# Gate and value products of a gated layer's second token half by Strassen's seven products, with their combinations on GpSimd

## Chip, cores and metric

The kernel runs on one core of a Trainium2 chip. The metric is the device time of one launch in microseconds (us); the kernel before takes 1157.8 us (median of three runs, 1156.64 to 1159.02). Engines go by the profile's names: PE (TensorE matmuls), PEld (its weight loads), DVE (VectorE), ACT (ScalarE), POOL (GpSimd) and SP (SyncE, which here only issues DMAs).

## What is computed

Attention over 4 x 12 heads of 448 x 64, then a layer of eight experts with a sorted routing, then a gated layer. The change is in the last one; its input x has 1792 tokens of 768.

```python
def _moe2_ref(x, w_gate, w_val, w_out) -> np.ndarray:
    gate = 1.0 / (1.0 + np.exp(-(x @ w_gate)))
    val = x @ w_val
    return (gate * val @ w_out).astype(np.float32)
```

The gate and value matrices are 768 x 1536, the output matrix is 1536 x 768.

## The kernel before, in words

**Precision.** A float32 operand is split in a high and a low part of a format that PE reads fast. `prods` takes a list of pairs of such operands and issues three matmuls for each (high x high, high x low, low x high), all into one PSUM bank. The operand ahead in a pair is stationary (128 x 128), the other streams (448 tokens, or 384 output columns).

**Gated layer.** `moe2(hf)` runs twice, for a half of 896 tokens each, that is two blocks of 448. For each of `NF` = 12 weight blocks `f` (128 columns of gate and of value) and each token block it makes the gate by 18 matmuls (6 depth tiles x 3) into a bank `pg`, ACT's sigmoid `gv`, the value by 18 matmuls into `pv`, DVE's product (L875), and the high and low part of that product `h` in `hx` (ACT L877, DVE L878). After every second `f` comes the output stage: for 7 token tiles and two column halves each 6 matmuls of 384 columns (3 for each of the two `f`), and DVE adds the bank to `acc` (L899; for the first pair ACT copies it). At the last pair GpSimd scatters the rows to the output.

**Weights.** `load_chunk` brings the weights in the order of the list `chunks`: gate and value of one `f` are one chunk ("gv"), the output weights of two `f` another ("wo"). A chunk's high and low part lie in `wh` and `wl`, four buffers each. In the first half the inputs are 64-bit numbers: `conv_half` loads half a chunk (`cs`, two buffers), ACT and DVE turn it into float32 (`ca`, two buffers, DVE L87 to L92) and split it (ACT L93, DVE L94), and SP stores both parts in a DRAM scratch `wsc` (L711, L712). In the second half SP only reads them back (L708, L709).

**Second half's tokens.** They come out of the experts as float32 (`X2F`), and `split2` splits them (ACT L914, DVE L915) at the end of the first half.

**Order.** PE's order is that of the code. The order on the other engines is made at build time by a scheduler; each engine executes its own list strictly in that order, and SP's DMAs are issued in SP's. PSUM has seven banks `g` for this part. Buffers rotate, and a writer waits until the last reader of the buffer's earlier content has ended.

```python
            for bb in range(2):
                x2h, x2l = X2[2 * hf + bb]
                xx = [(x2h[:, d, :], x2l[:, d, :]) for d in range(KD)]
                pg = ps.tile([128, 512], F32, name="g", bufs=7)
                prods(pg[:, :448], list(zip(wv[:KD], xx)))
```

Of the kernel before, what the change touches and what calls it, by code (L numbers as in the profile page):

```python
# [7 lines left out]
F32 = mybir.dt.float32  # L8
# [14 lines left out]
KD = 6  # L23
# [7 lines left out]
def body(ctx: ExitStack, tc: tile.TileContext, q, k, v, moe_w_gate, moe_w1, moe_w2,  # L31
# [12 lines left out]
    x_d = dram.tile([N, DM], F32, name="x_d")  # L44
    idx_d = dram.tile([N, 1], I32, name="idx_d")
# [19 lines left out]
    def conv_half(kind, f, n, hn, ln):  # L65
        cs = cv.tile([128, HC, 2], U32, name="cs", bufs=2)
        with tc.issue_after(xst[-1]):
            conv_load(kind, f, n, cs)
        conv_split(cs, hn, ln)
# [8 lines left out]
    def conv_split(cs, hn, ln):  # L78
# [15 lines left out]
        nc.vector.tensor_tensor(ln, w_, hn.bitcast(F32), op=OP.subtract)  # L94

# [573 lines left out]
    WB = 4  # L669

    def load_chunk():
# [3 lines left out]
        if kind in ("w1", "w2") and a in SPLIT:  # L675
            wh_, wl_ = (mp.tile([128, CH], F32R, name=n, bufs=WB) for n in ("wh", "wl"))
# [9 lines left out]
        if kind in ("w1", "w2"):  # L686
            full = mp.tile([128, CH], F32, name=("wh", "wl")[stream["next"] % 2], bufs=WB)
# [11 lines left out]
        hi = mp.tile([128, CH], F32R, name="wh", bufs=WB)  # L699
        lo = mp.tile([128, CH], F32R, name="wl", bufs=WB)  # L700
        o_ = wsc[wsc_n[kind, c]]
        for n in range(2):
            cc = slice(n * HC, (n + 1) * HC)
            if a == 0:
                with tc.issue_after(marks[E - 2].ins):
                    conv_half(kind, c, n, hi[:, cc], lo[:, cc])
# [3 lines left out]
        if a == 0:  # L710
# [3 lines left out]
        stream["next"] += 1  # L714

# [71 lines left out]
    def moe(ph, nxt):  # L787
# [35 lines left out]
        if half == 0:  # L823
            if blk < 2:
                X2[blk] = [mp.tile([128, KD, 448], F32R, name=n, bufs=2) for n in ("x2h", "x2l")]
            else:
                X2F[blk] = mp.tile([128, KD, 448], F32, name="x2f", bufs=2)
        xo = slice(half * CAP, (half + 1) * CAP)
        ws = [use(("w2", ph, c)) for c in range(2)]
        for dp in range(0, KD, 2):  # L830
# [25 lines left out]
    def moe2(hf):  # L856
        NT = 7
# [3 lines left out]
        for f in range(NF):  # L861
            wh, wl = use(("gv", hf, f))
# [3 lines left out]
            for bb in range(2):  # L866
                x2h, x2l = X2[2 * hf + bb]
                xx = [(x2h[:, d, :], x2l[:, d, :]) for d in range(KD)]
# [7 lines left out]
                gv = pv[:, :448]  # L876
                nc.scalar.activation(hx[:, 0, bb], gv, AF.Copy)  # L877
                nc.vector.tensor_tensor(hx[:, 1, bb], gv, hx[:, 0, bb].bitcast(F32), op=OP.subtract)  # L878
            gs.append(hx)
            if f % 2 == 1:  # L880
                oh, ol = use(("wo", hf, f - 1))
                if f == NF - 1:
                    nc.gpsimd.dma_start(idxf, idx_d[hf * 896:(hf + 1) * 896].rearrange("(t p) o -> p (t o)", p=128))
                    if hf == 0:
                        split2()
                for tt in range(NT):
                    for dh in range(2):
                        po = ps.tile([128, 512], F32, name="g", bufs=7)
                        pr = []
                        for n, hx in enumerate(gs):  # L890
                            a = [hx[:, t].rearrange("p b c -> p (b c)")[:, tt * 128:(tt + 1) * 128] for t in range(2)]
                            b_ = [t[:, n * 768 + dh * 384:n * 768 + dh * 384 + 384] for t in (oh, ol)]
                            pr.append((a, b_))
                        prods(po[:, :384], pr)
                        ac = acc[:, tt, dh * 384:(dh + 1) * 384]
                        if f == 1:
                            nc.scalar.activation(ac, po[:, :384], AF.Copy)
                        else:
# [59 lines left out]
```

## Time and profile before

| What | Value |
|---|---|
| time, median of 3 runs | 1157.8 us |
| time of the profiled execution | 1157.51 us |
| its span (first to last instruction) | 1155.3 us |
| PE busy | 1111.0 us (96% of the span), 7509 matmuls |
| DVE busy | 634.7 us (55%) |
| ACT busy | 394.4 us (34%) |
| POOL busy | 118.9 us (10%) |
| mean granted clock of TensorE | 0.983 |
| bytes moved by DMA | 180.63 MB, mean 156 GB/s |

The profile is that of one execution. Its span is 2.2 us shorter than that execution's time, and that time is 0.3 us under the median. The gated layer takes up the last 46% of the span: its first half lies at 617.8 to 883.2 us, its second half at 883.2 to 1148.9 us.

### The profile page before, as it was taken

What the parts mean: (1) busy time and instruction counts of PE and PEld (TensorE: products, weight loads), DVE (VectorE), ACT (ScalarE), POOL (GpSimd) and SP (SyncE); (2) the same over time, 40 slices, a digit from 0 to 9 for tenths busy, and PEclk for the clock granted to TensorE, in tenths of its full rate; (3) what the DMA queues carried; (4) which work ended last, traced back from release to release, by engine and by line L of the source; (5) the groups of instructions that cost most, each with busy time, mean ns of one, the idle gap of its engine ahead of it and who ended that gap; (6) DMA issues with size and microseconds to landing.
All of it is one profiled execution on the core that took longest, in us unless ns stands there. A gap on an engine that the chain in (4) does not pass through costs nothing.

```text
span 1155.3 us, 19791 instructions
## 1 busy us (share of the span) xinstructions
PE 1111.0 (96%) x7509; PEld 1038.1 (90%) x7509; DVE 634.7 (55%) x1902; ACT 394.4 (34%) x755; POOL 118.9 (10%) x231
## 2 busy tenths in 40 slices
PE   6999999963999999999999999999999999999997
PEld 6999999952888998899999999999999999999997
DVE  5777777765554555451558978868624113223223
ACT  4767676730110110122546754344221210110100
POOL 6333333200000000000000000000002000000002
PEclk9999999985999999999999999999999999999999
DMA  8555565335856666766557986565235333333302
GB/s 169 121 148 142 138 152 145 97 103 120 238 151 167 134 165 166 167 193 175 161 165 262 315 297 219 203 234 218 110 109 205 110 110 110 109 109 109 109 1 95
DMA packets 159582, 180.63 MB, mean 156 GB/s; under 512 B 74864, under 2 KB 140416, under 8 KB 159488
## 3 DMA queue, kind: packets, MB, share of 16 engines
q1 hardware_dynamic: 156064, 168.11, 47.3%
q0 software_dynamic: 2496, 11.04, 5.3%
q8 instruction: 59, 0.97, 0.4%
q14 instruction: 35, 0.29, 0.1%
q10 hardware_dynamic: 928, 0.23, 0.1%
HBM read 129.01 MB, written 39.33 MB: 146 GB/s over the span
## 4 chain that ended last, share of the span: by engine, by line
PE 94%; DMA 3%; DVE 2%; issue 1%; POOL 0%; SPq 0%; POOLq 0%; ACT 0%; DVEq 0%
PE g L735 71%; PE o L342 8%; PE w L322 4%; PE s L289 2%; PE s L290 2%; DMA xg<-x_d,ids 2%; PE w L251 2%; PE r L497 2%; PE g L777 1%; PE w L380 1%; PE w L363 1%; DMA st<-lo 1%; PE r L510 0%; DMA qt<-in_q_dram 0%; DVE cmp L492 0%
## 5 line engine op out<-in xcount | busy, mean ns | idle before, releaser
L735 PE MATMUL g<-x2l,wh 128*128 128x448 f32 x576 | 211.8, 368 | 0.0
L735 PE MATMUL g<-x2h,wl 128*128 128x448 f32 x576 | 211.8, 368 | 0.0
L735 PE MATMUL g<-x2h,wh 128*128 128x448 f32 x576 | 211.8, 368 | 0.0
L735 PE MATMUL g<-wh,hx 128*128 128x384 f32 x672 | 172.5, 334 | 0.0
L875 DVE TENSOR_TENSOR g<-g,gv 128x448 f32<-128x448 f32 x48 | 30.3, 632 | 205.9 <-PE g L735 202.6
L735 PEld LDWEIGHTS g<-wh,hx 128*128 128x128 f32 x672 | 121.5, 188 | 0.2
L735 PEld LDWEIGHTS g<-x2h,wl 128*128 128x128 f32 x576 | 108.1, 188 | 10.7
L735 PEld LDWEIGHTS g<-x2h,wh 128*128 128x128 f32 x576 | 108.1, 188 | 10.5
L735 PEld LDWEIGHTS g<-x2l,wh 128*128 128x128 f32 x576 | 108.1, 188 | 10.4
L735 PE MATMUL g<-wl,hx 128*128 128x384 f32 x336 | 112.2, 334 | 0.0
L342 PE MATMUL o<-vt,pt 112*112 112x65 f32 x960 | 106.3, 258 | 0.0
L342 PEld LDWEIGHTS o<-vt,pt 112*112 112x112 f32 x960 | 101.9, 178 | 0.0
L735 PE MATMUL g<-hx,wh 128*128 128x224 f32 x480 | 99.5, 328 | 0.0
L899 DVE TENSOR_TENSOR acc<-g,acc 128x384 f32<-128x384 f32 x140 | 75.8, 555 | 38.7 <-PE g L735 35.8
L300 ACT ACTIVATE sm<-sm,mn 112x112 f32<-112x112 f32 (+1 forms) x192 | 90.3, 522 | 3.9 <-DVE mn L292 3.9
L292 DVE CUSTOM_DVE_ANT_0 sm<-s,mask 112x112 f32<-112x112 f32 (+1 forms) x192 | 78.5, 445 | 22.7 <-PE s L290 22.5
L735 PE MATMUL g<-xx,wh 128*128 128x224 f32 x384 | 90.9, 344 | 0.0
L735 PE MATMUL g<-hx,wl 128*128 128x224 f32 x384 | 89.3, 336 | 0.0
L735 PE MATMUL g<-xx,wl 128*128 128x224 f32 x384 | 87.4, 338 | 0.0
L872 ACT ACTIVATE gv<-g 128x448 f32<-128x448 f32 x48 | 26.1, 544 | 169.0 <-PE g L735 168.9
L735 PEld LDWEIGHTS g<-hx,wh 128*128 128x128 f32 x480 | 80.8, 191 | 1.2
L735 PEld LDWEIGHTS g<-hx,wl 128*128 128x128 f32 x384 | 72.0, 190 | 0.6
(195 smaller groups left out, 1694.4 us busy)
## 6 DMA issues: line engine op xcount, KB each, us to landing
wh<-in_moe_w_dram SPq DMA_DIRECT2D x48, 384.0 KB, 3.7
wl<-in_moe_w_dram SPq DMA_DIRECT2D x48, 384.0 KB, 5.3
wsc<-wh SPq DMA_DIRECT2D x18, 768.0 KB, 3.4
wsc<-wl SPq DMA_DIRECT2D x18, 768.0 KB, 5.9
wl<-wsc SPq DMA_DIRECT2D x36, 384.0 KB, 3.8
wh<-wsc SPq DMA_DIRECT2D x36, 384.0 KB, 4.4
raw<-in_moe_w_dram SPq DMA_DIRECT2D x32, 384.0 KB, 3.7
cs<-in_moe_w_gate_dram SPq DMA_DIRECT2D x12, 768.0 KB, 4.9
```

Source lines behind the costliest of these rows:

```text
L251: nc.tensor.transpose(tr[:, c, :], t[:, c].rearrange("p h d -> p (h d)"), ident[:P, :P])
L289: nc.tensor.matmul(ss[j], qq[:, j, qs], kh[:, j, :w], start=True, stop=False)
L290: nc.tensor.matmul(ss[j], QZ[u % NZ][:, j, qs], kl[:, :w], start=False, stop=True)
L292: nc.vector.tensor_tensor_reduce(sm[:, j, :w], ss[j], mask[:, S - w:], op0=OP.add, op1=OP.min, scale=1.0, scalar=3.0e38, accum_out=mn[:, j ...
L300: nc.scalar.activation(sm[:, j, :w], sm[:, j, :w], AF.Exp, bias=mn[:, j:j + 1], scale=-1.0)
L322: nc.tensor.transpose(w[:P, n, :], sm[:, j, c * P:(c + 1) * P], ident[:P, :P])
L342: nc.tensor.matmul(o[:, n, j, :], pt[:, j * (i + 1) + c, :], vt[:, j, c, :], start=c == 0, stop=c == i)
L497: nc.tensor.matmul(c[:, :J], oha[:, tt_, :], cmps[2 * tt_ // T][:, tt_ % (T // 2), :J], start=tt_ == 0, stop=tt_ == T - 1)
L735: nc.tensor.matmul(o, a, b, start=first, stop=last_)
L872: nc.scalar.activation(gv, pg[:, :448], AF.Sigmoid)
L875: nc.vector.tensor_tensor(pv[:, :448], pv[:, :448], gv, op=OP.mult)
L899: nc.vector.tensor_tensor(ac, po[:, :384], ac, op=OP.add)
```

## The change

The second half's gate and value are no longer made block by block. Two weight blocks (`f`, `f` + 1), the two depth halves (3 depth tiles each) and the two token blocks form a 2 x 2 by 2 x 2 product of blocks, which is made from seven products of sums instead of eight products (Winograd's form of Strassen's scheme).

- `moe2` becomes `moe2a` (first half, as before) and `moe2b`. A unit of `moe2b` is one of gate (`n` = 0) or value (`n` = 1) of a pair of blocks: seven products of 9 matmuls each, in the order 1, 6, 5, 7, 3, 2, 4. Seven additions on DVE (L1020, L1022, L1023, four at L1011) join them to the four results. `m1`, `u2`, `u3` in the text are the buffers `ca`, `ca`, `k3`.
- `combine` makes the weight sums for a unit: GpSimd makes four sums or differences (L746 to L751) of the float32 weights in `cs`, ACT takes the high part of each of the seven (L739), GpSimd the low one (L740): 11 GpSimd and 7 ACT operations of 128 x 384 for each of 12 units. The parts fill four buffers `w`.
- `stage` (in the middle of the first half) and `stage_parts` (at its end) make the token sums: three GpSimd operations of 128 x 1344, a fourth in `stage_parts`, and seven times ACT and DVE on 128 x 1344 for the parts. `split2` goes.
- The second half's tokens go through DRAM: two stores of `X2F` to `x2_d` (L895), four loads (L970).
- In the first half SP stores, for gate and value, the float32 `ca` of each half chunk (L717, 24 stores of 384 KB) in place of both parts (L711 and L712, 24 stores of 768 KB). In the second half it loads that (L732) in place of both parts. Output weights stay as they were.
- `wh` and `wl` become one pool `w` of eight. The output stage takes the token tiles as 4, 5, 6, 3, 0, 1, 2 in the second half (tiles 4 to 6 lie in token block 1, tile 3 in both).

PE's list is the same up to the second half. What follows there is 756 instead of 864 matmuls of 448 columns; the 504 of the output stage stay.

```diff
+    x2_d = dram.tile([2, 128, KD, 448], F32, name="x2_d")
...
-    for hf in range(2):
-        for f in range(0, NF, 2):
-            chunks += [("gv", hf, f), ("gv", hf, f + 1), ("wo", hf, f)]
+    for f in range(0, NF, 2):
+        chunks += [("gv", 0, f), ("gv", 0, f + 1), ("wo", 0, f)]
+    for f in range(0, NF, 2):
+        chunks += [("s0", 1, f), ("s1", 1, f), ("wo", 1, f)]
...
-    WB = 4
+    WB = 8
+    def wt(dt=F32R):
+        return mp.tile([128, CH], dt, name="w", bufs=WB)
...
+        if kind in ("s0", "s1"):
+            W[chunks[stream["next"]]] = combine(int(kind[1]), c)
+            stream["next"] += 1
+            return
+        hi, lo = wt(), wt()
...
+                    w_ = conv_half(kind, c, n, hi[:, cc], lo[:, cc])
+                if kind == "gv":
+                    nc.sync.dma_start(o_[:, 0, cc], w_)
...
+        if a == 0 and kind == "wo":
...
+    def combine(n, f):
+        raw = cv.tile([128, HC, 2], U32, name="cs", bufs=2).rearrange("p f t -> p (f t)").bitcast(F32)
+        for e in range(2):
+            nc.sync.dma_start(raw[:, e * 768:(e + 1) * 768], wsc[wsc_n["gv", f + e]][:, 0, n * 768:(n + 1) * 768])
+        a11, a12, a21, a22 = (raw[:, i * 384:(i + 1) * 384] for i in range(4))
+        tl = [(wt(), wt()) for _ in range(2)]
+        got = {}
+        def parts(m, src, t, s_):
+            hi, lo = (x[:, s_ * 384:(s_ + 1) * 384] for x in tl[t])
+            nc.scalar.activation(hi, src, AF.Copy)
+            nc.gpsimd.tensor_tensor(lo, src, hi.bitcast(F32), op=OP.subtract)
+            got[m] = (hi, lo)
+        TT = nc.gpsimd.tensor_tensor
+        parts(1, a11, 0, 0)
+        parts(4, a22, 0, 1)
+        TT(a22, a21, a22, op=OP.add)
+        parts(5, a22, 0, 2)
+        TT(a21, a11, a21, op=OP.subtract)
+        TT(a11, a22, a11, op=OP.subtract)
+        parts(6, a11, 0, 3)
+        TT(a22, a12, a11, op=OP.subtract)
+        parts(7, a21, 1, 0)
+        parts(3, a22, 1, 1)
+        parts(2, a12, 1, 2)
+        return got
...
+        if blk >= 2 and half:
+            nc.sync.dma_start(x2_d[blk - 2], X2F[blk])
+    def xq():
+        return mp.tile([128, 3, 448], F32R, name="xq", bufs=8)
...
+    def stage():
+        b11, t2, t1, t3, b22, b21 = (xs(F32) for _ in range(6))
+        for t, kh, bb in ((b11, 0, 0), (t3, 0, 1), (b22, 1, 1), (b21, 1, 0)):
+            nc.sync.dma_start(t, x2_d[bb][:, 3 * kh:3 * kh + 3])
+        TT = nc.gpsimd.tensor_tensor
+        TT(t1, t3, b11, op=OP.subtract)
+        TT(t2, b22, t1, op=OP.subtract)
+        TT(t3, b22, t3, op=OP.subtract)
+        XR.update({1: b11, 6: t2, 5: t1, 7: t3, 3: b22, 2: b21})
+    XS = {}
+    def stage_parts():
+        t4 = cv.tile([128, HC, 2], U32, name="cs", bufs=2).rearrange("p f t -> p (f t)").bitcast(F32)
+        XR[4] = t4[:, :3 * 448].rearrange("p (c t) -> p c t", c=3)
+        nc.gpsimd.tensor_tensor(XR[4], XR[2], XR[6], op=OP.subtract)
+        for m in (1, 6, 5, 7, 3, 2, 4):
+            hi, lo = xq() if m == 1 else xs(), xq()
+            nc.scalar.activation(hi, XR[m], AF.Copy)
+            nc.vector.tensor_tensor(lo, XR[m], hi.bitcast(F32), op=OP.subtract)
+            XS[m] = (hi, lo)
...
+    def moe2b():
+        idxf = m2.tile([128, NT], I32, name="idxf", bufs=1)
+        acc = m2.tile([128, NT, DM], F32, name="acc", bufs=1)
+        stage_parts()
+        m1, u2, u3 = (cv.tile([128, HC], dt, name=nm, bufs=b).bitcast(F32)[:, :448]
+                      for dt, nm, b in ((U32, "ca", 2), (U32, "ca", 2), (U32, "k3", 1)))
+        of = o1.rearrange("p t c -> p (t c)").bitcast(F32)
+        sgs = [m2.tile([128, 448], F32, name="gv", bufs=2) for _ in range(2)] + [of[:, :448], of[:, 448:]]
+        for f in range(0, NF, 2):
+            hx = [mp.tile([128, 2, 2, 448], F32R, name="hx", bufs=3) for _ in range(2)]
+            for n in range(2):
+                qd = use((f"s{n}", 1, f))
+                def prod(m):
+                    o = ps.tile([128, 512], F32, name="g", bufs=7)[:, :448]
+                    prods(o, [tuple((t[0][sl], t[1][sl]) for t, sl in ((qd[m], (slice(None), slice(d * 128, (d + 1) * 128))),
+                                                                      (XS[m], (slice(None), d))))
+                              for d in range(3)])
+                    return o
+                def done(o, add, e, bb):
+                    V.tensor_tensor(o, o, add, op=OP.add)
+                    sg = sgs[2 * e + bb]
+                    if n == 0:
+                        nc.scalar.activation(sg, o, AF.Sigmoid)
+                    else:
+                        V.tensor_tensor(o, o, sg, op=OP.mult)
+                        h_parts(hx[e], bb, o)
+                nc.scalar.activation(m1, prod(1), AF.Copy)
+                V.tensor_tensor(u2, prod(6), m1, op=OP.add)
+                p5 = prod(5)
+                V.tensor_tensor(u3, prod(7), u2, op=OP.add)
+                V.tensor_tensor(u2, p5, u2, op=OP.add)
+                done(p5, u3, 1, 1)
+                done(prod(3), u2, 0, 1)
+                done(prod(2), m1, 0, 0)
+                done(prod(4), u3, 1, 0)
+            out_stage(1, f, hx, acc, idxf, (4, 5, 6, 3, 0, 1, 2))
...
+    moe2a()
+    moe2b()
```

DVE's list at the end of a pair of the second half, before: rows from the last value block of a pair and the first output tiles. `g` followed by a number is a PSUM bank's tile, `hx_12059` the parts of h.

```order
L875 TENSOR_TENSOR g_12081<-g_12081,gv_12079 128x448
L878 TENSOR_TENSOR hx_12059<-g_12081,hx_12059 128x448
L875 TENSOR_TENSOR g_12124<-g_12124,gv_12122 128x448
L899 TENSOR_TENSOR acc_10439<-g_12153,acc_10439 128x384
L878 TENSOR_TENSOR hx_12059<-g_12124,hx_12059 128x448
```

DVE's list in the same place of the change, in the value unit of the second pair. `g_10965`, `g_10991`, `g_11005`, `g_11019` are the banks of products 5, 3, 2 and 4, `hx_10809` and `hx_10810` the parts of h of the pair's first and second weight block.

```order
L1022 TENSOR_TENSOR k3_10464<-g_10975,ca_10463 128x448
L1023 TENSOR_TENSOR ca_10463<-g_10965,ca_10463 128x448
L1011 TENSOR_TENSOR g_10965<-g_10965,k3_10464 128x448
L1011 TENSOR_TENSOR g_10991<-g_10991,ca_10463 128x448
L1016 TENSOR_TENSOR g_10965<-g_10965,o1_80 128x448
L1016 TENSOR_TENSOR g_10991<-g_10991,gv_10466 128x448
L1011 TENSOR_TENSOR g_11005<-g_11005,ca_10462 128x448
L932 TENSOR_TENSOR hx_10810<-g_10965,hx_10810 128x448
L1016 TENSOR_TENSOR g_11005<-g_11005,gv_10465 128x448
L1011 TENSOR_TENSOR g_11019<-g_11019,k3_10464 128x448
L932 TENSOR_TENSOR hx_10809<-g_10991,hx_10809 128x448
L1016 TENSOR_TENSOR g_11019<-g_11019,o1_80 128x448
```

Before, two operations stood behind a block's last product. Now the addition of product 4 (`g_11019`, the unit's last product) stands ahead of the low part of product 3's h (`hx_10809<-g_10991`), which the first output tile reads. In the last pair these two stand the other way round.

ACT's list in the same value unit. `w_11156` and `w_11158` are the weight parts of the next pair's gate unit, `w_11263` those of its value unit.

```order
L1019 ACTIVATE ca_10462<-g_10943 128x448
L739 ACTIVATE w_11156<-cs_11153 128x384 x2
L931 ACTIVATE hx_10810<-g_10965 128x448
L739 ACTIVATE w_11158<-cs_11153 128x384 x3
L931 ACTIVATE hx_10809<-g_10991 128x448
L739 ACTIVATE w_11263<-cs_11260 128x384 x2
L931 ACTIVATE hx_10809<-g_11005 128x448
L931 ACTIVATE hx_10810<-g_11019 128x448
```

Before, only sigmoids and high parts of h stood here in turn. Now weight parts, which wait for GpSimd's sums, stand ahead of each of the first three high parts of h.

SP's list where the first converted weights are stored, before and then after. `ei7` is a routing result, `cs` a loaded half chunk.

```order
L73 DMA cs_8265<-in_moe2_w_gate_dram 128x6x256
L674 TENSOR_LOAD ei7_135
L674 ISA x2
L73 DMA cs_8278<-in_moe2_w_val_dram 128x6x256
L725 ISA
```

```order
L74 DMA cs_8272<-in_moe2_w_gate_dram 128x6x256
L680 TENSOR_LOAD ei7_136
L680 ISA x2
L717 DMA wsc_63<-ca_8161 128x768
L74 DMA cs_8286<-in_moe2_w_val_dram 128x6x256
L717 DMA wsc_63<-ca_8175 128x768
L766 ISA
```

Two stores, each of which waits for DVE, now stand ahead of the expert weights' loads (L766, L725 before); the stores of the same chunk stood much later.

## Rows read from the trace of the kernel before

**Rows 1.** Critical chain and PE's waits from 300 us: start or total, us, what.

```profile
583.08 563.04 PE g L735 x3030
...
PE g L777 <- DMA xg<-x_d,ids: 0.9, 1, 0.9
```

**Rows 2.** Windows: length, busy us (xcount) of PE, PEld, DVE, ACT, POOL; clock, DMA, GB/s.

```profile
0.00:60.00 60.00, 50.38 (x439) 47.73 (x440) 39.76 (x159) 35.89 (x79) 29.75 (x80) 1.00 0.66 143
617.77:883.15 265.38, 265.38 (x1370) 249.62 (x1369) 197.72 (x291) 118.00 (x174) 6.03 (x6) 1.00 0.62 219
883.15:1148.90 265.75, 265.75 (x1369) 249.41 (x1368) 68.52 (x118) 32.99 (x62) 7.71 (x8) 1.00 0.29 100
883.15:912.90 29.75, 29.75 (x145) 27.04 (x145) 4.33 (x7) 3.82 (x7) 1.95 (x2) 1.00 0.40 133
912.90:927.47 14.57, 14.57 (x85) 14.56 (x84) 1.26 (x2) 6.83 (x14) 0.00 (x0) 1.00 0.30 108
```

**Rows 3.** Groups by form, second half: xcount | busy us, mean ns | idle before.

```profile
L735 PE MATMUL g<-x2h,wh 128*128 128x448 f32 x288 | 106.0, 368 | 0.0
...
L899 DVE TENSOR_TENSOR acc<-g,acc 128x384 f32<-128x384 f32 x70 | 39.0, 558 | 30.7 <-PE g L735 28.7 <-issue 1.4 <-DVE acc L899 0.5
...
L877 ACT ACTIVATE hx<-g 128x448 fp32r<-128x448 f32 x24 | 13.1, 546 | 92.2 <-DVE g L875 92.2
```

**Rows 4.** Timeline at a value block's end: start us, us, engine, what.

```profile
1119.42 0.37 PE L735 MATMUL g<-x2h,wl 128*128 128x448 f32 x1
...
1119.62 0.37 PE L735 MATMUL g<-x2h,wh 128*128 128x448 f32 x1
...
1119.88 0.63 DVE L875 TENSOR_TENSOR g<-g,gv 128x448 f32<-128x448 f32 x1 [5.57 <-PE g L735]
...
1121.13 0.62 DVE L878 TENSOR_TENSOR hx<-g,hx 128x448 fp32r<-128x448 f32 x1 [0.61 <-ACT hx L877]
```

**Rows 5.** Timeline of DVE: three operations of 448 columns in a row.

```profile
549.26 1.69 DVE L782 TENSOR_TENSOR xl<-g,xx 128x448 fp32r<-128x448 f32 x3 [5.13 <-ACT xx L780]
```

**Rows 6.** POOL's groups by form, whole span.

```profile
L262 POOL CAST st<-hi 64x448 fp32r<-64x448 f32 x96 | 53.5, 558 | 134.5 <-ACT hi L257 120.1 <-DMA kt<-in_k_dram 11.3
...
L416 POOL TENSOR_TENSOR wg<-wr,wg 128x48 fp32r<-128x48 f32 x1 | 0.3, 287 | 0.1
...
L415 POOL CAST wg<-wr 128x48 fp32r<-128x48 f32 x1 | 0.2, 223 | 0.1
```

**Rows 7.** Single lines L262 and L292 (ns min/median/max), and L292's widest form by group.

```profile
L262 POOL CAST st<-hi x96: 551/560/562, 7.6 to 223.9; 64x448 fp32r<-64x448 f32 x96
...
L292 DVE CUSTOM_DVE_ANT_0 sm<-s,mask x192: 264/446/626, 11.6 to 237.9; 112x112 f32<-112x112 f32 x48, 112x224 f32<-112x224 f32 x48, 112x336 f32<-112x336 f32 x48, 112x448 f32<-112x448 f32 x48
...
L292 DVE CUSTOM_DVE_ANT_0 sm<-s,mask 112x448 f32<-112x448 f32 x48 | 28.0, 622 | 0.8 <-PE s L290 0.8
```

**Rows 8.** Timelines of DVE and SP where the first weights are converted.

```profile
500.99 0.93 DVE L92 SCALAR_TENSOR_TENSOR ca<-sq,ca 128x768 f32<-128x768 f32 x1
...
502.25 0.98 SPq L725 DMA_DIRECT2D wh<-in_moe_w_dram  x2
```

**Rows 9.** SP's stores of the second to fourth chunk, and line L94 (first and last start).

```profile
621.32 0.33 SPq L711 DMA_DIRECT2D wsc<-wh  x1
...
630.46 0.33 SPq L711 DMA_DIRECT2D wsc<-wh  x1
...
640.55 0.33 SPq L711 DMA_DIRECT2D wsc<-wh  x1
...
L94 DVE TENSOR_TENSOR wl<-ca,wh x36: 947/952/961, 609.4 to 826.5; 128x768 fp32r<-128x768 f32 x36
```

**Rows 10.** DMA issues from 560 us: xcount, KB each, median us to landing.

```profile
wsc<-wl SPq DMA_DIRECT2D x18, 768.0 KB, 5.9
...
wl<-wsc SPq DMA_DIRECT2D x36, 384.0 KB, 3.8
```

**Rows 11.** Timeline of DVE at the first half's end.

```profile
861.40 0.63 DVE L875 TENSOR_TENSOR g<-g,gv 128x448 f32<-128x448 f32 x1 [5.57 <-PE g L735]
...
874.01 0.62 DVE L878 TENSOR_TENSOR hx<-g,hx 128x448 fp32r<-128x448 f32 x1
```

More of the change, by code (lines that the diff above doesn't have):

```diff
@@ L68, in conv_half @@
             conv_load(kind, f, n, cs)
[L69 removed]
+        return conv_split(cs, hn, ln)
     def conv_load(kind, f, n, cs):
@@ L675, in load_chunk @@
         if kind in ("w1", "w2") and a in SPLIT:
-            wh_, wl_ = (mp.tile([128, CH], F32R, name=n, bufs=WB) for n in ("wh", "wl"))
+            wh_, wl_ = wt(), wt()
             for n in range(2):
@@ L686, in load_chunk @@
         if kind in ("w1", "w2"):
-            full = mp.tile([128, CH], F32, name=("wh", "wl")[stream["next"] % 2], bufs=WB)
+            full = wt(F32)
             for n in range(2):
@@ L824, in moe @@
             if blk < 2:
-                X2[blk] = [mp.tile([128, KD, 448], F32R, name=n, bufs=2) for n in ("x2h", "x2l")]
+                X2[blk] = [[xq() for _ in range(2)] for _ in range(2)]
             else:
-                X2F[blk] = mp.tile([128, KD, 448], F32, name="x2f", bufs=2)
+                X2F[blk] = mo.tile([128, KD, 448], F32, name="x2f", bufs=2)
         xo = slice(half * CAP, (half + 1) * CAP)
@@ L866, in moe2 @@
             for bb in range(2):
-                x2h, x2l = X2[2 * hf + bb]
-                xx = [(x2h[:, d, :], x2l[:, d, :]) for d in range(KD)]
+                x2h, x2l = X2[bb]
+                xx = [(x2h[d // 3][:, d % 3, :], x2l[d // 3][:, d % 3, :]) for d in range(KD)]
                 pg = ps.tile([128, 512], F32, name="g", bufs=7)
@@ L886, in moe2 @@
[L886 to L898, printed above, removed]
-                            nc.vector.tensor_tensor(ac, po[:, :384], ac, op=OP.add)
-                    if f == NF - 1:
-                        s_ = nc.gpsimd.indirect_dma_start(
-                            out=out, out_offset=bass.IndirectOffsetOnAxis(ap=idxf[:, tt:tt + 1], axis=0),
-                            in_=acc[:, tt, :], in_offset=None)
-                        for o_ in scats:
-                            tc.declare_no_dep(s_.ins, o_.ins, reason="other rows")
-                        scats.append(s_)
@@ L907, in moe2 @@
-                gs = []
-    def split2():
-        for blk in (2, 3):
-            X2[blk] = [mp.tile([128, KD, 448], F32R, name=n, bufs=2) for n in ("x2h", "x2l")]
-            for d in range(KD):
-                x2h, x2l = (t[:, d] for t in X2[blk])
-                nc.scalar.activation(x2h, X2F[blk][:, d], AF.Copy)
-                nc.vector.tensor_tensor(x2l, X2F[blk][:, d], x2h.bitcast(F32), op=OP.subtract)
+                out_stage(0, f - 1, gs, acc, idxf, range(NT))
+                gs = []
@@ L926, in body @@
     m2 = ctx.enter_context(tc.tile_pool(name="m2", bufs=2))
-    for hf in range(2):
-        moe2(hf)
+    moe2a()
+    moe2b()
 _INS = ['q', 'k', 'v', 'moe_w_gate', 'moe_w1', 'moe_w2', 'moe2_w_gate', 'moe2_w_val', 'moe2_w_out']
```

55 lines of the change are left out of this document (39 added, 16 removed).

## The prediction, made blind

> **What bounds the kernel now.** I read the critical chain first. It is one row of PE's matmuls from 583.08 us on, 563.04 us long and without a break [rows 1]; in the same stretch PE waits for other work for 0.9 us in all [rows 1]. In the windows both halves of the gated layer show PE busy for their whole length, 265.38 of 265.38 and 265.75 of 265.75 us [rows 2]. In the second half DVE is busy for 68.52 us, ACT 32.99, POOL 7.71, and the DMA engines have a share of 0.29 [rows 2]. So the time from 583 us is PE's list, matmul by matmul, and each other engine has room for three times its present work and more. The granted clock is 1.00, the 2.4 GHz level, in both halves [rows 2]. Two windows give the prices: of a pair of weight blocks, the gate and value part (144 matmuls of 448 columns) takes 29.75 us and the output stage (84 of 384) 14.57 us [rows 2], which is 206.6 and 173.4 ns for each matmul. A pair takes 44.3 us. (The 368 ns of a group's row [rows 3] is the duration of one matmul, with its overlap; the pitch counts.)
>
> **What is removed from PE.** A pair's gate and value go from 144 to 14 products of 9, that is 126 matmuls. Shape and operand type stay, so the price stays: 18 x 0.2066 = 3.72 us less per pair, 40.6 instead of 44.3. For six pairs **-22.3 us**.
>
> **A wait that is added.** Before, PE left the gate and value part with the newest block's h unfinished, and it cost nothing. At a value block's end the next group of matmuls begins at 1119.62, the product (L875) at 1119.88, 0.26 us later, and the low part (L878) lasts from 1121.13 to 1121.75, so h is whole 2.1 us after the block's last matmul [rows 4]. The first tiles of the output stage read token block 0, whose value part had ended 36 matmuls or 7.4 us earlier, and PE went on.
>
> Now the first output tile is tile 4, of token block 1, and its third matmul reads the low part that comes from product 3. Set a value unit's start to 0. A product takes 9 x 0.2066 = 1.86 us, so product 5 ends at 5.58, 7 at 7.44, 3 at 9.30, 2 at 11.16 and 4 at 13.02. DVE reacts 0.26 us after a group's end [rows 4] and executes one operation of 448 columns each 0.56 us when they stand in a row (three in 1.69 us [rows 5]; a single one lasts 0.62 [rows 4]). Its list in the order shown gives these starts: L1022 7.70, L1023 8.26, L1011 for product 5 8.82, L1011 for product 3 9.56, both L1016 10.12 and 10.68, L1011 for product 2 11.42, L932 for product 5 11.98, L1016 for product 2 12.54. Next in the list is L1011 for product 4, which cannot start before 13.02 + 0.26 = 13.28. Behind it stands L932 for product 3: it starts at 13.84 and ends at 14.46. PE wants it at 13.02 + 2 x 0.173 = 13.37. PE thus waits about 1.1 us. In the last pair the two operations stand the other way round: product 3's low part starts at 13.10 and ends at 13.72, and PE waits about 0.4 us. The tiles of block 0 come 3 x 2.08 us later, by when product 4's low part (L1016 14.4, ACT's high part of 0.55 us [rows 3], low part to about 16) is there. Sum **+5.9 us** (5 x 1.1 + 0.4). Bounds: nothing, if DVE gets to product 3's low part before product 4 ends, to 12 us, if the reaction and the two operations behind it cost twice what I take. I expect no loss of clock by these gaps: in the first 60 us PE stands idle for 9.6 us and the granted clock is 1.00 [rows 2].
>
> **GpSimd's weight sums.** No row of before shows a GpSimd operation of this size. Its cast of 128 x 48 takes 223 ns and that of 448 columns 558 ns [rows 6]: 0.84 ns a column and 0.18 us fixed. Its one two-input operation, 48 columns, takes 287 ns [rows 6]: the same fixed part leaves 2.17 ns a column, so 384 columns take **1.02 us**. The low bound is the cast's slope, 0.50 us, the high one eight times the whole 48-column operation, 2.3 us. I take 1.02, the row of the same operation. A pair has 22 of them, 22.4 us of 41.7: half loaded. A unit's sums start when its buffer `cs` comes free, about one unit ahead, and nothing on PE wants them before the next unit.
>
> What can go wrong is ACT, whose list now has weight parts (L739) ahead of high parts of h. ACT waits there for GpSimd. The second group of L739 (parts 5 and 6) needs six GpSimd operations; it starts about 0.65 us into the value unit and must be done, with its own 0.5 us and a handover of 0.25, before the high part for product 5 is wanted at about 10.7: 0.65 + 6T + 0.73 < 10.7, T < 1.55 us. Below that it costs nothing; above it, h is late by six times the excess in each unit, until at T = 44.3/22 = 2.0 us GpSimd alone is as slow as the old pair. At 2.3 us a pair takes 22 x 2.3 = 50.6 us, 6.3 more than before.
>
> The Trainium skill (GPSIMD Engine Reference, 3.1 and 4.1) speaks against the edit: it tells to give plain elementwise work to VectorE, since GpSimd takes about twice as long for it (4497 ns for a two-input operation of 2048 columns). An estimate from that figure is 0.84 us for 384 columns, by which the sum would be the same. POOL's 7.71 busy us here are why I think that the rule doesn't decide.
>
> **First half.** SP stores 24 times 384 KB in place of 24 times 768 KB and adds four loads and two stores of the tokens; the bytes fall by some 4 MB. New is that `ca`, of which there are two, is held until its store has landed. A store of 768 KB took 5.9 us to land and a transfer of 384 KB 3.8 [rows 10]. Chunks were converted about 9.6 us apart at first (stores at 621.32, 630.46, 640.55 [rows 9]); with a whole landing of 3.8 us added to that a chunk takes 13.4 us, and PE uses one in 265.4/18 = 14.7 us [rows 2]. The last conversion (L94) started at 826.5 [rows 9], and PE was at work on the half's chunks until 883. The stream gets slower but stays ahead: **0**. If landings take 5.9 us, a chunk takes 15.5 us, and 0.8 us on each of 12 chunks is lost: bound 10 us. On SP's queue two stores, waiting for DVE's L92, come ahead of the expert weights' loads; L92 ended at 501.92 and those loads were issued at 502.25 [rows 8], so their wait is over: 0.
>
> **Between the halves.** `split2`'s 24 operations of 448 columns become seven of 1344 on ACT and seven on DVE, about 1.4 us each, and one GpSimd operation of 0.18 + 1344 x 2.17 ns = 3.1 us. They start at about 861, behind the product of the last weight block's first token block (L875 at 861.40 [rows 11]), one part after another, and end at about 886. The seventh is wanted at 883.2 + 6 x 1.86 = 894.3. Free of cost, but the low part of the last h (874.01 [rows 11], wanted by tile 3 at about 874.8) now stands behind several of them on DVE: **+0.5 us**, bounds 0 and 5, once.
>
> **Sum.** 1157.5 - 22.3 + 5.9 + 0.5 = 1141.6 on the profiled execution, whose time is 0.3 us under the median; I say **1141.5**. The tail behind PE's last matmul (L899 and the scatter) is as before.
>
> **Rivals.**
>
> *The whole saving, no wait.* If the low part of product 3 is there in time, the time is 1157.5 - 22.3 = 1135.2. For it: PE's waits in before are 0.9 us in all. Against it: the order of DVE's list, which can't be overtaken.
>
> *Something in the feed stalls PE besides.* GpSimd operations of 1.6 to 1.8 us, weight chunks late in the first half, or the token parts late: some 2 to 12 us once or in sum, so 1143.5 to 1154. For it: these prices are the unseen ones. Against it: the margins above are several us each, and the 48-column row would have to be wrong by half.
>
> *GpSimd becomes the bound (the other side).* With T at 2.0 us or more the pair is GpSimd's, and the kernel is slower than before: at 2.3 us 1157.5 + 6 x 6.3 = 1195. It decides from T = 2.0. For it only the bound speaks, since the large share of a small operation's time may not be fixed; against it the casts, where 448 columns took only 2.5 times as long as 48.
>
> *DVE and GpSimd block each other.* If each DVE operation had to wait for GpSimd's running one, DVE's chain at a unit's end would lengthen by up to five times 1.02 us; PE would wait 5 us more per pair, 1171.5. In before, GpSimd's L262 took 551 to 562 ns in all of 96 cases though DVE's L292 (622 ns mean, 626 at most) ran in the same stretch, so neither was lengthened [rows 7]. The Trainium skill (SBUF — State Buffer, "Who interferes with whom") names one case in which they do block: a DVE operation with two inputs in SBUF against a GpSimd operation that reads SBUF. DVE's operations in the second half all have one input in PSUM, except the token parts between the halves; by that rule only the 0.5 us there would grow, within its bound of 5.
>
> **How the numbers follow.** Forecast (1138 to 1145): 0.65. Whole saving (1135 to 1138): 0.10. Feed stalls (1145 to 1155): 0.17. At or above 1155.5: 0.08, of which 0.03 within 0.2% (2.3 us, about what a measurement of this kernel can tell from no change) and 0.05 above, the two last rivals together. The range 1136 to 1150 leaves out about half of the second case (0.05), a third of the third (0.06) and the last (0.08). Faster 0.92, same 0.03, slower 0.05.
>
> **What would show it.** PE: 126 matmuls in 26.0 us and a pitch of 206.6 ns still; a wait of about 1.1 us at the first output tile of pairs 1 to 5, released by DVE's L932, and about 0.4 in the last. POOL: L740 and L746 to L751 at about 1.02 us; ACT's L739 released by POOL, but L931 not late. No wait of PE for weights or tokens, and stores L717 landing before the next L87 wants `ca`. The prediction is wrong if PE's waits in the second half are released by POOL or a DMA, if a GpSimd operation takes more than 1.55 us, or if PE's granted clock falls behind the gaps.

## The result, and the profile after

The changed kernel took 1139.24 us (median of 4 runs, 1138.34 to 1144.44), the kernel before 1157.22; the ratio is 0.985 [0.982, 0.989]. The prediction said 1141.5, range 1136 to 1150. The profiled execution took 1139.49 us with a span of 1137.7.

I read the windows first, as for [rows 2]. The columns are the same; the rows are a gate and value part and an output stage of the first pair of the second half, the last output stage, and the second half up to its last matmul. Ahead of them stands a gate and value part of the first half.

```profile
662.52:692.28 29.76, 29.76 (x146) 27.04 (x145) 26.77 (x36) 18.44 (x27) 0.00 (x0) 1.00 0.79 275
884.12:909.73 25.61, 25.61 (x127) 23.46 (x126) 13.44 (x22) 9.22 (x20) 19.28 (x20) 1.00 0.59 201
909.73:925.48 15.75, 14.97 (x86) 14.65 (x86) 2.90 (x6) 9.07 (x19) 9.61 (x10) 1.00 0.16 50
1116.43:1131.25 14.82, 14.68 (x85) 14.36 (x83) 9.82 (x19) 1.09 (x2) 5.75 (x6) 1.00 0.34 133
884.12:1131.25 247.13, 243.09 (x1261) 228.48 (x1260) 118.67 (x206) 72.16 (x148) 124.70 (x126) 1.00 0.26 87
```

The second half falls from 265.75 [rows 2] to 247.13 us, 18.6 less. A pair's gate and value take 25.61 in place of 29.75, that is 4.14 us less and not the 3.72 of 18 matmuls: the 126 that are left follow one another by 203.3 ns (their pitch, or cadence), those of the first half still by 206.7 in every pair behind an output stage. Five output stages take 15.75 in place of 14.57 us, the last 14.82 (14.99 with its last matmul), so 6 x 4.14 - 5 x 1.17 - 0.42 = 18.6. PE came to the second half 1.0 us later than before, and the tail is the same: the span is 17.6 us shorter.

Within the second pair, the nine matmuls of product 1 and the 117 that follow:

```profile
925.48:927.33 1.85, 1.85 (x10) 1.69 (x10) 0.00 (x0) 1.73 (x4) 1.23 (x2) 1.00 0.00 0
927.33:951.09 23.76, 23.76 (x119) 21.77 (x117) 10.06 (x17) 7.39 (x16) 10.93 (x12) 1.00 0.31 100
```

These are 206 and 203.1 ns for each: product 1 still has the longer cadence, and from product 6 on the stream has the shorter one.

Of PE's waits from 300 us on one row is left (total, times, longest), and it is the predicted one:

```profile
PE g L776 <- DVE hx L932: 3.9, 5, 0.8
```

DVE's timeline at the end of the fourth pair's value unit, which began at 1020.96 (start, length in us):

```profile
1028.47 0.62 DVE L1022 TENSOR_TENSOR k<-g,ca 128x448 f32<-128x448 f32 x1 [2.97 <-PE g L776]
...
1033.20 0.62 DVE L1016 TENSOR_TENSOR g<-g,gv 128x448 f32<-128x448 f32 x1
1033.95 0.63 DVE L1011 TENSOR_TENSOR g<-g,k 128x448 f32<-128x448 f32 x1
1034.49 0.61 DVE L932 TENSOR_TENSOR hx<-g,hx 128x448 fp32r<-128x448 f32 x1
```

Counted from the unit's start these are 7.51, 12.24, 12.99 and 13.53 us; the prediction had 7.70, 12.54, 13.28 and 13.84. PE's own timeline shows the hole between the second and the third matmul of the output stage:

```profile
1033.77 0.61 PE L776 MATMUL g<-w,hx 128*128 128x384 f32 x2
1035.16 1.16 PE L776 MATMUL g<-w,hx 128*128 128x384 f32 x5 [0.78 <-DVE hx L932]
```

GpSimd's operations, single lines (ns min/median/max), and then ACT in the same unit: the weight part that waits for GpSimd's difference (L749) ends at 1028.30, and the first high part of h starts at 1031.50. The margin of 3.2 us is the one that the prediction's terms give.

```profile
L740 POOL TENSOR_TENSOR w<-cs,w x84: 996/1014/1046, 840.4 to 1093.4; 128x384 fp32r<-128x384 f32 x84
```

```profile
1027.77 0.53 ACT L739 ACTIVATE w<-cs 128x384 fp32r<-128x384 f32 x1 [2.52 <-POOL cs L749]
1031.50 0.55 ACT L931 ACTIVATE hx<-g 128x448 fp32r<-128x448 f32 x1 [3.20 <-DVE g L1016]
```

One thing was not in the prediction. In the first half DVE's L93 and L95 take up to 3.85 us; the same operations took 0.93 (an L92, [rows 8]) and at most 0.96 (L94, [rows 9]) before. They lie beside `stage`'s three GpSimd sums, which ran at 637.8 to 649.2 us, at the end of the first pair's products and not in the middle of the half, where their code stands. DVE's timeline, then POOL's, in the same stretch:

```profile
637.69 0.95 DVE L95 TENSOR_TENSOR w<-ca,w 128x768 fp32r<-128x768 f32 x1
638.56 3.85 DVE L93 SCALAR_TENSOR_TENSOR ca<-sq,ca 128x768 f32<-128x768 f32 x1
642.34 0.62 DVE L954 TENSOR_TENSOR g<-g,gv 128x448 f32<-128x448 f32 x1
643.33 2.87 DVE L95 TENSOR_TENSOR w<-ca,w 128x768 fp32r<-128x768 f32 x1 [0.37 <-ACT w L94]
```

```profile
637.77 3.83 POOL L972 TENSOR_TENSOR xs<-xs 128x1344 f32<-128x1344 f32 x1 [8.99 <-DMA xs<-x_d]
641.68 3.70 POOL L973 TENSOR_TENSOR xs<-xs 128x1344 f32<-128x1344 f32 x1
```

L93 ends 0.8 us after L972, L95 0.8 us after L973, and alone they take 0.95: these operations of DVE, with two inputs in SBUF, behave as if they started when GpSimd's ends. L954, with one input in PSUM, runs through L973 in its usual 0.62 us. The Trainium skill (SBUF — State Buffer, "Who interferes with whom") says just this, that such an operation and a GpSimd operation that reads SBUF exclude each other for the whole instruction; the traces agree.

### The profile page after: what moved, and what is told of

It reads as the page before. It is cut to its first block, busy times and chain, and to the rows that moved or that the text cites. A ratio compares the mean times of both kernels' runs of the same rounds, so it can differ in the third digit from the quotient of the medians.

```text
span 1137.7 us, 19889 instructions
## 1 busy us (share of the span) xinstructions
PE 1090.1 (96%) x7401; PEld 1019.3 (90%) x7401; DVE 696.9 (61%) x1981; ACT 441.8 (39%) x846; POOL 268.6 (24%) x367
## 4 chain that ended last, share of the span: by engine, by line
PE 94%; DVE 3%; issue 1%; POOL 1%; DMA 0%; POOLq 0%; SPq 0%; DVEq 0%
PE g L776 70%; PE o L344 8%; PE w L324 4%; PE s L291 3%; PE s L292 2%; PE r L499 2%; PE w L253 1%; PE g L818 1%; PE w L382 1%; PE w L365 1%; PE r L512 1%; DVE cmp L494 0%; DMA st<-lo 0%; DVE g L1011 0%; DVE hx L932 0%
## 5 line engine op out<-in xcount | busy, mean ns | idle before, releaser
L776 PE MATMUL g<-xq,w 128*128 128x448 f32 x1188 | 281.6, 367 | 0.0
L776 PEld LDWEIGHTS g<-xq,w 128*128 128x128 f32 x1188 | 222.7, 188 | 20.8
L776 PE MATMUL g<-w,hx 128*128 128x384 f32 x1008 | 179.0, 335 | 4.0 <-DVE hx L932 3.9
L776 PEld LDWEIGHTS g<-w,hx 128*128 128x128 f32 x1008 | 174.6, 188 | 7.3 <-DVE hx L932 5.9
L776 PE MATMUL g<-xx,w 128*128 128x224 f32 x768 | 155.2, 340 | 0.0
L776 PE MATMUL g<-hx,w 128*128 128x224 f32 x864 | 154.0, 331 | 0.0
L776 PEld LDWEIGHTS g<-hx,w 128*128 128x128 f32 x864 | 137.5, 190 | 1.7
L776 PEld LDWEIGHTS g<-xx,w 128*128 128x128 f32 x768 | 134.9, 191 | 1.9
L776 PE MATMUL g<-xs,w 128*128 128x448 f32 x432 | 124.7, 365 | 0.0
L740 POOL TENSOR_TENSOR w<-cs,w 128x384 fp32r<-128x384 f32 x84 | 83.5, 1016 | 126.4 <-ACT w L739 126.4
L739 ACT ACTIVATE w<-cs 128x384 fp32r<-128x384 f32 x84 | 40.0, 518 | 93.0 <-PE g L776 49.5
```

Of the source, the lines that this page charges most:

```text
L739: nc.scalar.activation(hi, src, AF.Copy)
L740: nc.gpsimd.tensor_tensor(lo, src, hi.bitcast(F32), op=OP.subtract)
L776: nc.tensor.matmul(o, a, b, start=first, stop=last_)
```

## The experiments

Three groups (e1 to e4, e5 to e8, e9 and e10), each on one chip with its own runs of the kernel before, whose medians were 1160.36, 1158.38 and 1158.81 us; so kernels of different groups compare by their ratios. Ratios to before, with 95% intervals:

| Run | Edit to the changed kernel | Median us | Ratio |
|---|---|---|---|
| e1_order | DVE's order | 1137.60 | 0.979 [0.977, 0.982] |
| e2_both | and the order of the weight blocks | 1134.88 | 0.978 [0.976, 0.980] |
| e3_kick_after | extra matmul, first half | 1139.88 | 0.981 [0.979, 0.984] |
| e4_kick_before | extra matmul, kernel before | 1154.90 | 0.995 [0.993, 0.997] |
| e5_after_again | none | 1142.39 | 0.984 [0.982, 0.987] |
| e6_dve | weight sums on DVE | 1154.73 | 0.995 [0.993, 0.997] |
| e7_lo2 | low parts twice | 1143.33 | 0.987 [0.984, 0.989] |
| e8_best | e2, e3 and short token sums | 1132.02 | 0.976 [0.974, 0.978] |
| e9_short_sums | short token sums | 1140.54 | 0.984 [0.983, 0.986] |
| e10_lo3 | low parts three times | 1189.74 | 1.028 [1.025, 1.030] |

**Is the wait DVE's order?**

```diff
-                    V.tensor_tensor(o, o, add, op=OP.add)
+                    with tc.issue_after(aft.ins) if aft is not None else ExitStack():
+                        V.tensor_tensor(o, o, add, op=OP.add)
...
-                done(prod(3), u2, 0, 1)
+                l3 = done(prod(3), u2, 0, 1)
...
-                done(prod(4), u3, 1, 0)
+                done(prod(4), u3, 1, 0, l3)
```

> Only DVE's list changes: in the value unit of pairs 1 to 5 the low part of product 3's h stands ahead of the addition of product 4, as it already does in the last pair. Theory of the prediction (PE waits at the first output tile because of this order on DVE): the output stages of pairs 1 to 5, 15.75 us each in the changed kernel, shrink to the 15.15 us of the last pair, so 5 x 0.6 = 3.0 us less, about 1136.2 us against 1139.2. Rival (the wait is set by ACT's high part of product 3's h, which stands behind three weight parts): the output stages stay at 15.75 us and the time at 1139.2.

```diff
-                for n, hx in enumerate(gs):
+                for n, hx in list(enumerate(gs))[::-1 if hf else 1]:
```

> The same order on DVE, and in the second half each output tile multiplies the pair's second weight block first, so that PE wants the low part from product 3 at its sixth matmul in place of its third, 0.52 us later. Theory of the prediction: no wait of PE is left, each output stage falls to 84 x 173.4 ns = 14.6 us, 6.4 us less than in the changed kernel in all, about 1132.8 us. Rival (the loss at the output stage is a fixed cost of starting on a token tile of the newest block, or of the change from 448 to 384 columns): the stages stay above 15.1 us and the time at 1136 or more.

The window of the first output stage in e1_order, then in e2_both:

```profile
911.62:926.60 14.98, 14.94 (x85) 14.62 (x85) 2.92 (x6) 8.99 (x19) 9.66 (x10) 1.00 0.17 53
```

```profile
910.50:925.08 14.58, 14.58 (x86) 14.58 (x84) 2.93 (x6) 9.04 (x19) 9.70 (x10) 1.00 0.18 55
```

All six stages are like these. The swap of two rows on DVE gives back 0.76 of 1.17 us, the later reading the rest: no wait is left. The theory holds, the rivals (ACT, a fixed cost) fall. The times say less: by their ratios the interval of e2_both lies wholly below that of the changed kernel, that of e1_order only touches it.

**Why 203 and not 207 ns?**

```diff
                 pg = ps.tile([128, 512], F32, name="g", bufs=7)
+                if f % 2 == bb == 0: mm(pg[:, :64], wv[0][0], xx[0][0][:, :64], True, True)
```

> One extra matmul of 64 columns at the start of each pair of the first half, into a bank that the next matmul starts anew. In the changed kernel the 448-column matmuls follow one another by 202.7 ns in the first pair of the first half and by 206.7 ns in the five pairs after an output stage, with the same code and the same tiles of tokens. Theory: PE keeps one of two cadences until something disturbs its stream, so the extra matmul brings 202.7 ns into pairs 2 to 6: 5 x (144 x 4.0 ns less about 0.1 us) = 2.4 us less, 1136.8 us. Rival (the cadence is set by where the operands lie, or by what else runs at that time): the pitch stays 206.7 and the six extra matmuls cost 0.6 us, 1139.8.

> The kernel before with the same extra matmul of 64 columns at the start of every pair of both halves. Theory of the two cadences: 11 pairs go from 206.7 to 202.7 ns a matmul, 11 x 0.48 = 5.2 us less, about 1152.2 us; then this much of the change's gain in the second half (2.5 us) has nothing to do with the seven products. Rival (operands' place or other work sets the pitch): 12 extra matmuls cost 1.2 us, about 1158.5.

The second pair's gate and value part of the first half in e3_kick_after, and the first of the second half in e4_kick_before:

```profile
666.70:695.99 29.29, 29.29 (x147) 27.15 (x146) 27.09 (x37) 18.54 (x27) 0.00 (x0) 1.00 0.81 275
```

```profile
881.45:910.75 29.30, 29.30 (x147) 27.16 (x146) 4.33 (x7) 3.81 (x7) 1.94 (x2) 1.00 0.41 135
```

29.29 us with one matmul more, in place of 29.75 [rows 2]: behind an output stage the shorter cadence comes with the small matmul, in stages that have no seven products, on the same tiles. The rival (operands' place, other work) falls.

In the first pair of the first half, which follows 224-column matmuls of the experts, it went the other way. That part in the changed kernel, in e5_after_again (the same program once more), and with the small matmul in e3_kick_after:

```profile
618.74:647.93 29.19, 29.19 (x146) 27.06 (x145) 25.95 (x28) 16.64 (x25) 11.08 (x4) 1.00 1.00 362
```

```profile
618.99:648.75 29.76, 29.76 (x146) 27.05 (x145) 27.21 (x25) 13.61 (x20) 11.52 (x4) 1.00 0.98 350
```

```profile
621.38:651.26 29.88, 29.88 (x148) 27.16 (x147) 26.78 (x27) 16.49 (x25) 12.22 (x4) 1.00 0.99 357
```

Without the small matmul the first pair had the shorter cadence in eight of nine profiles and the longer one in e5_after_again; with it, it had the longer one in all three (e3_kick_after, e4_kick_before, e8_best), 0.7 us lost. So one program can run in either, and a small matmul changes the cadence, not always to the shorter one.

In e4_kick_before all 11 parts behind an output stage take 29.29, which makes 5.1 us; less the 0.7 of the first pair this fits a span 4.3 us shorter, and the ratio agrees. So 2.5 us of the change's 18.6 come from a change of cadence that the kernel before could have had too. The median of e3_kick_after, 1139.88, is what the rival forecast, and its interval overlaps that of the changed kernel; only the windows decide there. In its profile the first pair took 0.7 us more by the cadence and its output stage 15.44 us, 0.85 late, which ate most of the gain.

**GpSimd or VectorE for the weight sums?**

> The changed kernel unchanged, as a base beside the kernels of this group on the same chip. The first measurement gave 0.985 of before and the account by stages says 1139.2; nothing else is expected: output stages of 15.7 us (15.0 in the last pair), 25.6 us for each pair's products.

```diff
-            nc.gpsimd.tensor_tensor(lo, src, hi.bitcast(F32), op=OP.subtract)
+            nc.vector.tensor_tensor(lo, src, hi.bitcast(F32), op=OP.subtract)
...
-        TT = nc.gpsimd.tensor_tensor
+        TT = nc.vector.tensor_tensor
```

> All 22 weight sums and low parts of a pair go from GpSimd to VectorE; PE's list stays. Theory of the prediction (GpSimd's 22.4 us a pair are off the path, and what counts is the order on VectorE at the end of a value unit): each operation takes about 0.46 us there in place of 1.02 (1.56 us x 384/1344), but three of them stand between the value unit's sums and product 3's low part, so PE waits about 1.0 us more at each of five output stages: about 5 us slower than the changed kernel, 1144. Rival (elementwise work belongs on VectorE, which does it in less than half the time): no slower than the changed kernel, 1139 or less, since ACT gets its weight parts earlier.

In e6_dve the first pair's output stage, and the stretch of it behind the wait (the column ahead of the last two is the granted clock); then the single line of the low parts and PE's waits in the second half:

```profile
911.05:929.50 18.45, 16.51 (x85) 16.18 (x85) 8.21 (x16) 8.94 (x19) 0.00 (x0) 0.91 0.13 43
913.89:917.06 3.17, 3.17 (x11) 3.17 (x11) 2.69 (x6) 0.57 (x2) 0.00 (x0) 0.50 0.61 235
```

```profile
L740 DVE TENSOR_TENSOR w<-cs,w x84: 545/548/560, 841.8 to 1107.4; 128x384 fp32r<-128x384 f32 x84
```

```profile
PE g L776 <- DVE hx L932: 9.7, 5, 1.9
```

An operation takes 0.55 us on VectorE and 1.01 on GpSimd, and VectorE loses, by 12 us (in the profiles five stages of 2.7 us and a start of the gated layer 1.1 us later, less 2.8 us that the base e5_after_again lost in its own first pair, below). The theory had the wait right (1.9 in place of 0.8 us) and its price wrong: each stage is 2.7 us longer and not 1.0, because behind the wait 10 or 11 matmuls ran at a granted clock of 0.50, the 1.2 GHz level, by 0.32 us each, 1.6 us more than at 0.173. The waits of 0.8 us in the changed kernel had left the clock at 1.00. The Trainium skill (GPSIMD Engine Reference, 4.1) gives elementwise work to VectorE, as the faster; faster it is here, by 1.85 times, and the wrong place all the same.

The length of a wait alone does not decide on the clock. The same trace has a sixth wait of 1.9 us, in the experts' part, and the 5 us behind it ran at 1.00:

```profile
PE g L818 <- DMA xg<-x_d,ids: 1.9, 1, 1.9
```

```profile
331.37:336.37 5.00, 5.00 (x41) 4.24 (x41) 1.62 (x7) 1.42 (x3) 0.00 (x0) 1.00 0.62 173
```

In e5_after_again the same program as the changed kernel was late in the first half. Its first output stage, and DVE's lines ahead of it:

```profile
648.75:665.59 16.84, 15.11 (x85) 14.47 (x84) 16.10 (x22) 14.94 (x27) 0.00 (x0) 1.00 0.56 193
```

```profile
637.98 3.83 DVE L90 CUSTOM_DVE_ANT_0 ca<-ca,k 128x1536 uint16<-128x1536 uint16 x1
641.74 3.84 DVE L95 TENSOR_TENSOR w<-ca,w 128x768 fp32r<-128x768 f32 x1
645.50 3.83 DVE L93 SCALAR_TENSOR_TENSOR ca<-sq,ca 128x768 f32<-128x768 f32 x1
649.25 0.62 DVE L954 TENSOR_TENSOR g<-g,gv 128x448 f32<-128x448 f32 x1
```

Three operations in a row stood behind GpSimd's three token sums, and the last block's product (L954) behind them: 2.3 us. PE's longest wait there, 1.3 us, left the clock at 1.00. Another 0.6 us of this profile's 3.1 over the first one is the longer cadence of the first pair, shown above.

**How much more can GpSimd bear?**

```diff
-            nc.gpsimd.tensor_tensor(lo, src, hi.bitcast(F32), op=OP.subtract)
+            for _ in range(2): nc.gpsimd.tensor_tensor(lo, src, hi.bitcast(F32), op=OP.subtract)
```

> GpSimd executes each low part twice (18 operations a unit in place of 11, 36.6 us a pair). Theory of the prediction (ACT's wait for GpSimd costs nothing until the six operations ahead of parts 5 and 6 take 10.7 - 0.65 - 0.73 = 9.3 us): they become nine, 9.1 us, just below; 18.3 us a unit is still under the 20.6 of PE. Within 1 us of the changed kernel, about 1139.5. Rival (GpSimd's work is already near what ACT and PE can bear): some 3 us a pair, 1155 or more, with PE's waits released through DVE's low parts.

> GpSimd executes each low part three times: 25 operations a unit, 50 x 1.016 = 50.8 us a pair, more than the 44.3 us that a pair took before. Theory of the prediction's rival (beyond the old pair's length GpSimd is the bound and the kernel is slower than before): pairs 2 to 6 take 50.8 us each in place of 41.3, 47 us in all less a head start of at most 10 us: 1177 to 1190. Other theory (ACT, held by GpSimd, also holds the first pair's h and PSUM banks, and PE's clock falls behind the long waits, which adds to it): over 1190.

In e7_lo2 the first pair's gate and value part with the wait behind it, and a stretch of the output stage:

```profile
885.50:914.87 29.37, 25.75 (x128) 23.46 (x127) 13.69 (x23) 9.16 (x19) 27.21 (x28) 1.00 0.53 175
...
915.14:919.14 4.00, 3.96 (x15) 3.64 (x15) 2.75 (x5) 3.00 (x7) 4.00 (x5) 0.61 0.01 4
```

ACT's timeline there:

```profile
909.60 0.53 ACT L739 ACTIVATE w<-cs 128x384 fp32r<-128x384 f32 x1 [8.67 <-POOL cs L746]
912.60 0.52 ACT L739 ACTIVATE w<-cs 128x384 fp32r<-128x384 f32 x1 [2.48 <-POOL cs L749]
913.03 0.53 ACT L931 ACTIVATE hx<-g 128x448 fp32r<-128x448 f32 x1
```

The median is within 1 us of e5_after_again, as forecast, but not in the way forecast. In the first pair, where GpSimd also issues the first half's scatters, ACT stood behind GpSimd, h came late, PE waited 3.6 us and then ran at a lower clock. In the other five pairs it cost nothing, and the scheduler, with other work to place, had put product 3's low part ahead of product 4's addition, so their stages took 14.98 us. In the profiles the first pair's loss of 4.6 us stands against 3.0 gained in four later stages and 2.8 that the base had lost. Only the five pairs speak for the threshold: they show that just below it nothing is lost, and no run shows where the loss begins.

In e10_lo3 the waits of PE in the second half, and all of it in a window:

```profile
PE g L776 <- POOL w L740: 39.0, 6, 11.2
```

```profile
883.64:1180.60 296.96, 257.41 (x1261) 239.52 (x1260) 119.19 (x209) 74.81 (x150) 274.46 (x281) 0.92 0.22 72
```

GpSimd is the bound: 49.5 us a pair, and 31 us slower than before. The median, 1189.74, lies at the border of the two theories' ranges, and both are in it: 39.0 of the 50 us added to the changed kernel's second half are waits for GpSimd, and the mean clock there fell to 0.92.

**Short token sums, and the best version.**

```diff
-        TT(t1, t3, b11, op=OP.subtract)
...
+        for o, a, b in ((t1, t3, b11), (t2, b22, t1), (t3, b22, t3)):
+            for d in range(3):
+                TT(o[:, d], a[:, d], b[:, d], op=OP.subtract)
```

> The changed kernel with one edit: the three token sums in the first half are nine GpSimd operations of 448 columns in place of three of 1344. In one profile of the changed kernel they cost nothing, in the other the first pair's output stage took 16.84 us in place of 14.57, with DVE's operations of two SBUF inputs beside them at up to 3.85 us in place of 0.95. Theory (such an operation of DVE waits for the whole GpSimd operation that is running, so shorter ones delay it less): DVE's longest is about 2 us, the first output stage 14.6 us, and the time 0 to 2 us less than the changed kernel's 1139 to 1142. Rival (the total of GpSimd's work counts, not the length of one operation): the first output stage is late by about 2 us in some executions still, and DVE's operations add up to the same loss.

> Together: the order on DVE and the second weight block first (no wait at the output stages, 6.4 us), the extra matmul of 64 columns in the first half (2.3 us), and the token sums in the first half as nine GpSimd operations of 448 columns in place of three of 1344. In the changed kernel DVE's operations with two SBUF inputs took up to 3.85 us in place of 0.95 beside the long ones; theory (either engine's operation holds the other's for its whole length): with the short ones DVE's longest is about 0.95 + 1.2 = 2.1 us, and no output stage of the first half is late. Sum 1139.2 - 6.4 - 2.3 = about 1130.5 us. Rival (DVE's long operations come from DMA traffic at that time): DVE's longest stays near 3.85 us and the first pair's output stage stays 0.85 us late, as in the kernel with the extra matmul alone.

The single line of L95 in e9_short_sums, and windows of e8_best (a pair of the second half, and a gate and value part of the first):

```profile
L95 DVE TENSOR_TENSOR w<-ca,w x36: 943/951/1907, 611.4 to 828.5; 128x768 fp32r<-128x768 f32 x36
```

```profile
882.24:907.84 25.60, 25.60 (x128) 23.64 (x128) 13.42 (x23) 9.21 (x20) 19.27 (x20) 1.00 0.59 201
907.84:922.42 14.58, 14.58 (x86) 14.58 (x84) 2.93 (x6) 9.00 (x19) 9.67 (x10) 1.00 0.18 55
662.84:692.13 29.29, 29.29 (x146) 27.16 (x146) 26.74 (x36) 18.44 (x26) 0.00 (x0) 1.00 0.78 268
```

Beside the short sums DVE's longest is 1.9 us, half of the 3.85 beside the long ones. The fourth token sum (L982, in `stage_parts`) stayed one operation of 1344 columns, and beside it DVE took 3.85 us in this same kernel; POOL's row and DVE's:

```profile
816.93 3.31 POOL L982 TENSOR_TENSOR cs<-xs 128x1344 f32<-128x1344 f32 x1 [165.07 <-DVE ca L89]
```

```profile
817.21 3.85 DVE L90 CUSTOM_DVE_ANT_0 ca<-ca,k 128x1536 uint16<-128x1536 uint16 x1
```

So it is the length of the GpSimd operation that counts, not DMA traffic. The time of e9_short_sums is that of the changed kernel. With the long sums the first output stage was late in two of eight profiles, with the short ones in neither of two: that it is now never late, so few can't show. The best version has no wait of PE in the gated layer and beats both kernels, 0.976 [0.974, 0.978]. The sum said 1130.5 and the median is 1132.02; the small matmul gave 1.6 us in its first half and not 2.3, since it put the first pair into the longer cadence.

## Why the prediction was right

- **Bound.** Right: the gain is PE's list, minus one wait. Every removed matmul counted in full.
- **-22.3 us.** Right in kind, short by 2.5: "shape and operand type stay, so the price stays" failed. The price was 203.3 ns, since the stream left the longer cadence from product 6 on; e3_kick_after and e4_kick_before show that a shorter cadence goes without the change.
- **+5.9 us.** 6.3 measured, at the place and through the operation named, and taken away by two changes of order (DVE's rows, and which weight block an output tile reads first), with no work removed. Its last-pair part too (0.42 for 0.4).
- **Clock.** Right for waits of 0.8 us. That it need not hold for longer ones came out in e6_dve (1.9 us) and e7_lo2 (3.6 us).
- **GpSimd at 1.02 us.** 1.01. The margin on ACT was 3.2 us, as its terms gave. "GpSimd becomes the bound" was a true mechanism without its condition; e10_lo3 made the condition and showed its price.
- **First half at 0.** Zero in the first profile, 2.3 us in the second, 0.85 in e3_kick_after. The stores were covered as argued, with no wait of PE for weights; what was overlooked is that `stage`'s GpSimd sums meet DVE's conversions, whose operations have two inputs in SBUF. The mutual blocking was weighed for the second half alone (where it did not show: L740 took 996 to 1046 ns) and for the token parts (L986: up to 3.47 us in place of 1.56, and PE did not wait).
- **Between the halves +0.5.** 0.

The sum against the profiled execution: 1141.6 - 2.5 + 0.4 - 0.5 + 1.0 (late start of the gated layer) - 0.4 (time outside the span) = 1139.6, where 1139.5 was measured.

The late start had no term in the prediction. In the ten profiles with the change the gated layer starts at 617.6 to 621.4 us, in the two without it (before, e4_kick_before) at 617.8 and 617.6. One difference holds for all of them, PE's wait ahead of its first matmuls on the experts' gathered tokens, at about 277 us: 5.8 and 6.4 us without the change, 6.9 to 8.9 with it. The row of before and that of the changed kernel ("issue" stands where the profile shows nothing that ended a wait):

```profile
PE g L777 <- issue: 5.8, 1, 5.8
```

```profile
PE g L818 <- issue: 6.9, 1, 6.9
```

Whether the change makes it longer, and what it costs on average, was not tested. So it also stays open which part of the changed kernel's scatter (1138.3 to 1144.4) comes from this start, which from the first half's lateness and which from the cadence of the first pair.

## What to carry to other kernels

Where PE is gapless, price a change in its list and in what its next consumer reads first: here two rows on an engine with 50% idle time took back a quarter of the gain, and a reorder without any work gave it back. Put new work on the engine with slack in the place where it stands in nobody's way, even if it is the slower one there; then look for the operations with which it excludes another engine, and keep those short. When the pitch of equal matmuls differs between stages of one trace, treat it as a term of its own.

## What the runs showed of the hardware

- The same 448-column matmuls follow one another by 206.7 or by about 203 ns, at one granted clock (1.00). Behind 384-column matmuls the longer cadence came and lasted for the 144 that follow; a 64-column matmul ahead of them, or the passage from product 1 to product 6, brought the shorter one. Behind the experts' 224-column matmuls the same program ran once in the shorter and once in the longer (29.19 and 29.76 us), and with the 64-column matmul the longer one came (29.88). Why, no run shows.
- Waits of 0.8 and 1.3 us left TensorE's granted clock at 1.00; behind waits of 1.9 us in the second half it was 0.50 for ten or eleven matmuls in each of five places, some 1.6 us each, while one wait of 1.9 us in the experts' part of the same trace left it at 1.00.
- A GpSimd operation of 1344 columns (3.1 us where it started first, in e5_after_again) held DVE operations with two SBUF inputs to 3.85 us in place of 0.95, and was itself held to 3.8.
